# Down product of seven token pairs in a seven-product form with shared block sums, under a new instruction order

## The chip, the cores and the metric

The kernel runs on one core of one Trainium2 chip. The metric is the device time of one execution in microseconds, median of several runs; smaller is better. A core has a matrix engine (TensorE, PE in the profile, its weight loads PEld), three engines for elementwise work (VectorE or DVE, ScalarE or ACT, GpSimd or POOL) and SyncE (SP), which in this kernel only issues DMAs. Each engine runs its own list of instructions in order; they meet through semaphores.

## The reference, cut to what matters

One transformer block on 2048 tokens of width 640, in bfloat16: a layer norm, linear attention with 32 heads of 20 (a learned feature map `w_phi`, softmax of plus and minus the scores), an output product, a residual, a second layer norm, and a gated bilinear feed-forward of width 1536 with a second residual.

```python
qkv   = layernorm(x) @ wqkv                       # 640 -> 3*640
phi_q = [softmax(q w_phi), softmax(-q w_phi)]     # per head; phi_k alike
kv, z = phi_k^T v, sum(phi_k)                     # per head, over the tokens
h     = x + ((phi_q kv) / (phi_q z + 1e-6)) @ wo
y     = layernorm(h)
out   = h + ((y @ w_gate) * (y @ w_up)) @ w_down  # 640 -> 1536 -> 640
```

The change is in the last product, `(...) @ w_down`, and in the order in which all the work is issued.

## The kernel before, in words

Tokens are worked in 16 tiles of 128. Everything is emitted as small *units*, each with a name; a unit holds one or several operations on one or several engines. The names that matter here:

- Loads on SP: `in` (seven in SP's list, in this order of the program: two loads of the key weights into `phiqT`, the transposed token tiles 0 and 1 into `xT`, the value weights into `Wp`, the transposed token tiles 2 and 3), `lT4` to `lT15` (the other transposed token tiles), `lx0` to `lx3` (the tokens untransposed, four tiles each), `lwq` (the query weights into the buffer that held the key weights), `t0` to `t4` (transposed query weights), `lwo`, `lg`, `lu`, `ld` (output, gate, up and down weights). Two further `in` loads are on ACT's list: the last two fifths of the key weights, and `Wrows` (the feature map).
- Preparation of weights: `wk` (transposes of the key weights on PE, ten PE operations, with copies on DVE and ACT), `x0` to `x4` (key weights times feature map), `wv` and `c0` to `c4` (value weights centred), `wm`, `wq`, `y0` to `y4` (the same for the queries).
- Per token tile: `s` (statistics of the layer norm, in batches named by their first tile: `s0` is tiles 0 and 1, `s2` is tiles 2 and 3, `s4`, `s8`, `s12` four tiles each), `k`/`K` (key features), `v` (values), `A` (the sums over tokens), `q`/`Q` (query features, two DMA transposes each), `n` and `h` (attention output, output product and second layer norm), `f` (gate and up product of one of 12 feature blocks for four tiles).
- The down product: tiles 0 and 1 by the plain product (`d0`, `d1`), the other fourteen tiles in seven pairs `Db.i` (group of four tiles b, pair i). A pair is a 2-by-2 block product (two token tiles; features 0 to 767 and 768 to 1535; output columns 0 to 319 and 320 to 639), done with seven block products of six matmuls each instead of eight. Before it, `S` units form sums of blocks of the activations on DVE (`block_sums`, line 1101) and `T` units form sums of blocks of `w_down` on POOL, once for the whole kernel (`weight_sums`, line 1086).

In `down_pair` (line 1131) products accumulate in four PSUM banks; ACT copies a bank out (`snap`, line 1159), POOL adds copies to one another and to the residual `x_all` (`padd`, line 1165), DVE makes the last addition into the output tile (`fin`, line 1170), and SP stores it (`store`, line 1176).

The order on each engine is written out in `ORDER` as a list of unit names, one list per engine. `place` (line 213) takes the head of each list in turn, assigns buffers and fills DMA rings of eight slots; an engine's instructions are emitted in exactly the order of its list, SP's DMAs too. A load may be given a landing time with `at=`; `place` then takes that number for its landing, whatever its position in the list:

```python
land = o.at or max(s + 2.3, fabric) + o.bytes
...
load_wnat(1, (0, 1), at=2.9)
load_wnat(1, (1, 3), at=5.05)
load_xT(0, 5.35)
load_xT(1, 5.95)
load_wv(0, 5, 9.15)
for t, at in ((2, 9.1), (3, 9.8)):
    load_xT(t, at)
```

No wait in the emitted program depends on those numbers; each operation waits for the semaphores of what it reads (`finish`, line 302). `lwq` overwrites what `wk` reads, so its DMA is issued once the last `wk` transpose has been done. All matmuls are emitted from one helper (line 604), plain loads from line 497, transposing DMAs from line 501.

Of the kernel before, what the change touches and what calls it, by code (L numbers as in the profile page):

```python
# [472 lines left out]

# [845 lines left out]
```

## Time and profile before

| | |
|---|---|
| time, median of 3 runs | 276.26 us (276.13 to 276.52) |
| profiled execution: span from first to last instruction | 274.3 us |
| profiled execution: its own time | the page gives the span alone |
| PE busy | 266.2 us, 97% of the span |
| DVE, ACT, POOL busy | 202.0, 145.9, 147.9 us |
| granted TensorE clock | full in all 40 slices |
| DMA | 28.61 MB, busiest up to 60 us |

A span is shorter than the time by what lies around the first and last instruction. The profile page lists busy time by engine, 40 slices of the span, the DMA queues, the chain of work that ended last, groups of instructions and DMA issues by kind. A row of the timeline is: start in us, length in us, engine, source line, operation, what it writes and reads, shape, how many instructions are merged in it, and the idle time before it with what ended that. SPq and ACTq are the instruction streams that issue DMAs; their rows give the time that issuing takes, and "to landing" is from the issue to the semaphore. Matmuls are pipelined, so the length of a merged row is longer than the pitch of its matmuls by the drain of the last.

### The profile page before, as it was taken

To read this page: it belongs to the slowest core of one execution; us is meant where nothing else is said; L and a number is where in the kernel's file an instruction comes from. 1 tells how busy PE (TensorE), PEld (TensorE's weight loads), DVE (VectorE), ACT (ScalarE), POOL (GpSimd) and SP (SyncE) were. 2 spreads that over 40 slices of the span, in tenths; PEclk is the share of its full clock that TensorE was granted. 3 is DMA by queue.
4 is the path that set the end of the run, shared out by engine and by line. 5 is a ranking of instruction groups with operands and counts; after the bars stand their busy time and mean duration, and the time that the engine had idled before them with its cause. 6 is when DMAs were issued, how large, how long until landed. Compare 5 with 4: busy or idle time off the path is not lost.

```text
span 274.3 us, 5648 instructions
## 1 busy us (share of the span) xinstructions
PE 266.2 (97%) x2217; PEld 181.0 (66%) x2229; DVE 202.0 (74%) x388; ACT 145.9 (53%) x270; POOL 147.9 (54%) x187
## 2 busy tenths in 40 slices
PE   8999999999999999999999999999999999999992
PEld 8777776767868788788645557754554654456771
DVE  2899999999999989999855958555544565316772
ACT  3469999999676964776273422143342312332430
POOL 5437999999842365624899511621035330024895
PEclk9999999999999999999999999999999999999999
DMA  7988899803275897555564242620015101000112
GB/s 195 284 150 196 136 302 399 290 2 53 55 107 115 255 200 118 114 100 69 83 130 22 50 84 50 143 50 0 0 24 98 48 0 50 1 0 25 50 49 72
DMA packets 67099, 28.61 MB, mean 104 GB/s; under 512 B 57600, under 2 KB 65792, under 8 KB 67072
## 3 DMA queue, kind: packets, MB, share of 16 engines
q1 hardware_dynamic: 66144, 27.90, 44.9%
q10 hardware_dynamic: 928, 0.35, 0.5%
q8 instruction: 17, 0.28, 0.5%
q14 instruction: 10, 0.08, 0.1%
HBM read 11.82 MB, written 2.62 MB: 53 GB/s over the span
## 4 chain that ended last, share of the span: by engine, by line
PE 83%; POOL 6%; DVE 4%; DMA 2%; issue 2%; SPq 1%; ACT 1%; POOLq 0%; DVEq 0%
PE ps L604 83%; POOL eq L1167 4%; DMA Wp<-in_A_wqkv_dram 2%; POOL t L1167 2%; DVE ps L872 1%; DVE Sq L934 1%; SPq L501 1%; ACT phik L880 1%; DVE Ssum L894 0%; PE ps L512 0%; DVE Rk L896 0%; POOLq L371 0%; DVE x_all L1039 0%; DVE Phi L984 0%; SPq L497 0%
## 5 line engine op out<-in xcount | busy, mean ns | idle before, releaser
L604 PE MATMUL ps<-phik,Wgu 128*128 128x512 bf16 (+1 forms) x588 | 107.8, 335 | 0.6
L604 PEld LDWEIGHTS ps<-phik,Wgu 128*128 128x128 bf16 x600 | 58.1, 98 | 42.5 <-DVE phik L1079 1.2
L604 PE MATMUL ps<-Wp,xT 128*128 128x320 bf16 (+3 forms) x522 | 76.6, 299 | 0.2 <-ACT phik L880 0.2
L604 PEld LDWEIGHTS ps<-Wp,xT 128*128 128x128 bf16 x522 | 49.8, 98 | 19.5 <-ACT phik L880 0.7
L1079 DVE TENSOR_TENSOR phik<-ps,gate 128x512 bf16<-128x512 f32 (+1 forms) x60 | 34.0, 576 | 36.4 <-PE ps L604 29.9
L1077 ACT ACTIVATE gate<-ps 128x512 bf16<-128x512 f32 (+1 forms) x60 | 30.0, 511 | 53.8 <-PE ps L604 44.7
L897 POOL TENSOR_TENSOR phik<-phik,Rk 128x1280 bf16<-128x1280 bf16 x16 | 37.6, 2363 | 3.8 <-DVE Rk L896 3.0
L1167 POOL TENSOR_TENSOR eq<-eq 128x320 f32<-128x320 f32 x15 | 13.2, 881 | 33.1 <-ACT eq L1161 32.6
L872 DVE TENSOR_REDUCE ps<-ps 128x1 f32<-128x640 f32 (+1 forms) x32 | 26.1, 821 | 0.9 <-PE ps L604 0.3
L1161 ACT ACTIVATE eq<-ps 128x320 f32<-128x320 f32 x27 | 11.8, 438 | 27.0 <-PE ps L604 27.0
L1110 DVE TENSOR_TENSOR xT<-phik 128x768 bf16<-128x768 bf16 x35 | 23.7, 698 | 3.1 <-PE ps L604 3.1
L934 DVE TENSOR_REDUCE Sq<-eq 128x66 f32<-128x1320 bf16 x16 | 24.2, 1513 | 0.0
L894 DVE TENSOR_REDUCE Ssum<-phik 128x64 f32<-128x1280 bf16 x16 | 23.4, 1468 | 0.4 <-ACT phik L880 0.4
L1057 POOL TENSOR_SCALAR vpe<-shc 128x1 f32<-128x1 f32 x14 | 2.7, 192 | 36.4 <-ACT junk L597 36.1
L946 POOL TENSOR_TENSOR eq<-eq,rq 128x660 bf16<-128x660 bf16 x16 | 21.0, 1314 | 1.2
L597 ACT ACTIVATE junk<-x_all,nmh 128x640 bf16<-128x640 bf16 x14 | 11.6, 827 | 16.0 <-DVE x_all L1053 15.9
L880 ACT ACTIVATE eq<-ps,nb,rs 128x300 bf16<-128x300 f32 (+2 forms) x26 | 17.0, 687 | 5.4 <-DVE nb L875 4.6
L941 POOL TENSOR_TENSOR rq<-Sq,rq 128x33 f32<-128x33 f32 x16 | 4.5, 283 | 24.4 <-DVE rq L940 24.4
L604 PE MATMUL ps<-xT 128*128 128x320 bf16 (+1 forms) x144 | 17.4, 266 | 0.0
L880 ACT ACTIVATE eq<-ps,nb,nrs 128x300 bf16<-128x300 f32 (+2 forms) x26 | 17.2, 693 | 0.0
L880 ACT ACTIVATE phik<-ps,nb,rs 128x640 bf16<-128x640 f32 x16 | 14.2, 890 | 2.7 <-DVE nb L875 2.6
L604 PEld LDWEIGHTS ps<-xT 128*128 128x128 bf16 x144 | 11.8, 98 | 3.9 <-DVE xT L1110 0.2
(110 smaller groups left out, 374.9 us busy)
## 6 DMA issues: line engine op xcount, KB each, us to landing
x_all<-in_A_x_dram SPq DMA_DIRECT2D x4, 640.0 KB, 10.5
out_dram<-outb SPq DMA_DIRECT2D x16, 160.0 KB, 1.8
Wgu<-in_B_w_gate_dram SPq DMA_DIRECT2D x1, 1920.0 KB, 10.4
Wgu<-in_B_w_up_dram SPq DMA_DIRECT2D x1, 1920.0 KB, 15.8
vaug<-in_B_w_down_dram SPq DMA_DIRECT2D x1, 1920.0 KB, 9.0
Wp<-in_A_wqkv_dram SPq DMA_DIRECT2D x1, 800.0 KB, 4.9
phiqT<-in_A_wqkv_dram SPq DMA_DIRECT2D x1, 800.0 KB, 6.6
Wo<-in_A_wo_dram SPq DMA_DIRECT2D x1, 800.0 KB, 6.0
```

The lines of the kernel that those rows point to most:

```text
L604: ins = e.matmul(o_, lhsT=l_, rhs=r_, start=s_, stop=p_, skip_group_check=True)
L872: g.op("DVE", lambda e: e.tensor_reduce(out=mx(), in_=src(), axis=AX.XY if len(src().shape) == 3 else AX.X, op=ALU.max, apply_absolute_val ...
L880: g.op("ACT", lambda e, s=s, sc=sc, to=to, of=of: e.activation(out=to(s), in_=of(), func=ACT.Exp, bias=nb[:, i:i + 1], scale=sc[:, t:t + 1 ...
L894: g.op("DVE", lambda e: e.tensor_reduce(out=Ssum[:, vs.i, :], in_=x, axis=AX.X, op=ALU.add), rd=R_phik[t], wr=vs.R, use=[vs], t=1.39, lat=1.5)
L897: g.op("POOL", lambda e: e.tensor_tensor(out=x, in0=x, in1=Rk[:, vr.i, :].unsqueeze(2).to_broadcast([P, 2 * H, DH]), op=ALU.mult), rd=vr.R ...
L934: g.op("DVE", lambda e: e.tensor_reduce(out=Sq[:, vs.i, :].rearrange("p (w g) -> p w g", w=NQ), in_=feat(0, NQ).rearrange("p w (g f) -> p ...
L946: return e.tensor_tensor(out=x, in0=x, in1=rq[:, vr.i, :].rearrange("p (w h) -> p w h", h=HW).unsqueeze(3).to_broadcast([P, NQ, HW, DH]), ...
L1077: g.op("ACT", lambda e: e.activation(out=gate[:, vg.i, 0:P * n], in_=PS[v.i][:, 0, 0:P * n], func=ACT.Copy), rd=[v.R[0]], wr=vg.R, use=[v, ...
L1079: g.op("DVE", lambda e: e.tensor_tensor(out=hhT[:, hb, ft, sl], in0=PS[v.i][:, 1, 0:P * n], in1=gate[:, vg.i, 0:P * n], op=ALU.mult), rd=[ ...
L1110: g.op("DVE", lambda e, k=k, x=x, y=y, op=op: e.tensor_tensor(out=SH[k][i], in0=part(x), in1=part(y), op=op), rd=rd, wr=[R_S[k][i]], t=0.6 ...
L1161: o = g.op("ACT", lambda e: e.activation(out=slot(x), in_=PS[v.i][:, bk, 0:HALF], func=ACT.Copy), rd=[v.R[bk]], wr=x.R, use=[v, x], after= ...
L1167: g.op("POOL", lambda e: e.tensor_tensor(out=slot(o_), in0=slot(a), in1=in1(), op=op), rd=a.R + r_, wr=o_.R, use=[o_, a] + ([y] if x is No ...
```

## The change

The seven products of a pair are formed from other block sums. Each pair has four sums of activation blocks instead of five, two of them made from another sum, and there are four sums of weight blocks instead of five, two of them made from another sum. A pair's results are accumulated in three PSUM banks across products, with copies taken on the way: four copies by ACT instead of five, each followed by one POOL addition of `x_all` (four POOL additions instead of six), and four last additions by DVE, each of which reads a bank and one copy. The second tile of the pair is stored before the first. The number of products (seven) and of matmuls (42) per pair is the same. The `S` and `T` buffers move within `xT` and `Wp`. The dummy activation that loads ACT's table now uses the `junk` buffer's pool.

All five lists in `ORDER` are new. In SP's list the seven `in` loads stand at places 7, 8, 14, 23, 25, 27 and 29 of the list instead of 1 to 7. In ACT's list the `Wrows` load stands behind a first `wk` copy, and the table activation behind `x4`. `d0` and `d1` stand on PE ahead of the second half of the group `f0`; the last pair is D3.0 instead of D3.1.

```diff
     "PE":
-        "warm wk wk wk wk wk wk wk wk wk wk s0 s0 x1 x1 x3 wv wv x2 x0 x0 s2 s2 x4 k0 k0 k0 k0 k0 k3 k1 wm v2 k2 s4 v0 s4 s4 s4 "
+        "warm wk wk wk wk wk wk wk wk wk wk s0 s0 x1 x1 x3 wv wv x2 x0 x0 x4 s2 s2 k0 k0 k0 k0 k0 k1 k3 wm k2 s4 s4 s4 s4 k7 k4 "
...
-        "D3.0 D2.1 D3.0 D2.1 D2.1 D3.0 D3.0 D3.0 D3.1 D3.0 D3.1 D3.0 D3.1 D3.1 D3.1 D3.1 D3.1",
+        "f3.10.0 D2.0 D2.0 f3.6.0 f3.4.0 f3.4.0 D2.0 D2.0 D2.0 D2.0 f3.6.0 D2.1 D2.0 D2.1 D2.1 D3.1 D2.1 D2.1 D2.1 D3.1 D2.1 D3.1 "
+        "D3.0 D3.1 D3.1 D3.1 D3.1 D3.0 D3.0 D3.0 D3.0 D3.0 D3.0",
     "DVE":
...
+        "f3.10.0 S2.0.3 D2.0 S2.1.0 f3.4.0 D2.0 f3.6.0 D2.0 S2.1.2 S3.0.0 D2.0 S3.0.2 S2.1.3 S3.0.3 S3.1.0 D2.1 S3.0.1 S3.1.2 "
+        "D2.1 D2.1 D2.1 S3.1.1 S3.1.3 D3.1 D3.1 D3.1 D3.1 D3.0 D3.0 D3.0 D3.0",
     "ACT":
-        "in in in wk wk wk x2 x0 x4 k0 k0 wm k3 k3 v2 k1 k1 v0 k2 k2 wq3 wq1 v3 k7 k7 v7 y2 k4 k4 s12 v5 s12 v4 s12 y0 k6 k6 k5 "
+        "in wk in wk wk x2 x0 x4 in s12 k0 k0 k1 wm wo1 k1 k3 k3 k2 k2 wq1 s12 v2 wo1 v3 k7 v7 k7 k4 k4 k6 v5 k6 wq3 v0 s12 v1 y4 "
...
     "SP":
-        "in in in in in in in lwq t4 lT7 lT4 t2 lT5 lT6 t3 t1 t0 lx3 lT10 lT15 lT9 lT11 lT8 lT13 lT14 lT12 lx0 lwo lg lu lx2 "
-        "lx1 Q0 Q0 Q1 Q1 Q2 Q2 Q3 Q3 Q5 n2 Q5 n3 Q7 Q7 ld Q4 Q4 h2 h3 n5 Q6 Q6 n7 Q8 n4 Q8 n6 Q10 Q10 Q9 n8 Q9 h4 h5 h7 h6 Q12 "
...
+        "lx3 t2 t4 lT5 lT6 lwo in in lwq lT4 t0 lT7 lx1 in t1 lT9 lT8 lT11 lT10 lT15 lT13 t3 in lT12 in lT14 in lu in lg Q0 lx0 "
+        "Q0 lx2 Q1 Q1 Q2 Q2 Q3 Q3 Q5 Q5 n2 n3 Q7 Q7 ld Q4 Q4 n7 Q6 Q6 Q8 Q8 h2 n5 n6 n4 Q10 Q10 n8 h3 h7 Q9 Q9 h5 Q14 Q14 h6 h4 "
...
-    R_T, R_S = regs(5), [regs(2) for _ in range(5)]
+    R_T, R_S = regs(4), [regs(2) for _ in range(4)]
...
-    g.op("ACT", lambda e: e.activation(out=junk[:, 0, 0:1], in_=ones[:, 0:1], func=ACT.Exp), rd=[R_one], wr=[R_tab], t=1.4)
+    g.op("ACT", lambda e: e.activation(out=junk[:, 0, 0:1], in_=ones[:, 0:1], func=ACT.Exp), rd=[R_one], wr=[R_tab],
+         use=[Buf(p_junk)], t=1.4)
...
     def weight_sums():
...
-        for k, (a, b, op) in enumerate(((0, 3, ALU.add), (1, 3, ALU.subtract), (2, 0, ALU.subtract), (0, 1, ALU.add), (2, 3, ALU.add))):
+        for k, (a, b, op) in enumerate(((1, 0, ALU.subtract), (3, 1, ALU.subtract), (3, (0,), ALU.subtract), (2, (2,), ALU.subtract))):
...
     def block_sums(b, i):
...
-        for k, (x, y, op) in enumerate(((0, 3, ALU.add), (2, 3, ALU.add), (0, 1, ALU.add), (2, 0, ALU.subtract), (1, 3, ALU.subtract))):
+        for k, (x, y, op) in enumerate(((2, 3, ALU.add), (0, 2, ALU.subtract), ((0,), 0, ALU.subtract), (1, (2,), ALU.subtract))):
...
+        def snap(v, bk, t, half):
             x = Buf(p_slot)
...
+            x.read = g.op("ACT", lambda e: e.activation(out=slot(x), in_=PS[v.i][:, bk, 0:HALF], func=ACT.Copy), rd=[v.R[bk]],
+                          use=[v, x], t=0.42, lat=0.55, **rw)
+            g.op("POOL", lambda e: e.tensor_tensor(out=slot(x), in0=slot(x), in1=x_all[:, t, c], op=ALU.add), rd=x.R + [R_h[t]],
+                 wr=x.R, use=[x], t=0.87)
+            return x
...
-        padd(s4, s4, s5, ALU.subtract)
-        padd(s5, s4, None, x=(t1, 0))
-        padd(s1, s1, s4)
-        padd(s1, s1, None, x=(t2, 1))
-        padd(s1, s1, c12)
-        padd(s1, s1, c21, ALU.subtract)
-        fin(v1, 0, o1_, t1, s5)
+        mm(v1, 0, raw(0), wraw(0), True, [v2])
+        a_ = snap(v1, 0, t1, 0)
+        mm(v2, 0, summed(0), wsum_(0), True)
+        d_ = snap(v2, 0, t2, 1)
+        mm(v1, 0, summed(2), wsum_(2), False)
+        b_ = snap(v1, 0, t1, 1)
+        mm(v1, 1, raw(1), wraw(2), True)
+        fin(v1, 1, o1_, 0, a_)
+        mm(v1, 0, summed(1), wsum_(1), False)
+        c_ = snap(v1, 0, t2, 0)
+        fin(v1, 0, o2_, 1, d_, [c_])
+        mm(v2, 1, raw(3), wsum_(3), True)
+        fin(v2, 1, o2_, 0, c_)
+        store(o2_, t2)
+        mm(v2, 0, summed(3), wraw(3), False)
+        fin(v2, 0, o1_, 1, b_)
         store(o1_, t1)
-        fin(v2, 1, o2_, t2, s1)
-        store(o2_, t2)
...
-    g.alias(R_T, R_Wp[1] + R_Wp[2] + R_xT[0:6])
+    g.alias(R_T, R_Wp[1] + R_Wp[2] + R_xT[0:3])
...
-    g.alias([r for x in R_S for r in x], R_xT[5:])
+    g.alias([r for x in R_S for r in x], R_xT[2:12])
```

More of the change, by code (lines that the diff above doesn't have):

```diff
@@ L58 @@
 ST_ACT = (12,)
+SNAP = {}
 SPLIT = [[(0, 2), (2, 2)], [(0, 4)], [(0, 4)], [(0, 4)]]
@@ L143, in __init__ @@
         self.R = [Reg() for _ in range(nreg)]
+        self.read = None
 class Op:
@@ L465, in _build @@
     Wkv = Wp[:, :, D:3 * D]
-    TW = [Wkv[:, 0:3, 0:2 * HALF], Wkv[:, 0:3, 2 * HALF:4 * HALF], Wkv[:, 3:5, 0:3 * HALF],
-          xTf[:, 0:KH * HALF].rearrange("p (a n) -> p a n", a=3), xTf[:, KH * HALF:2 * KH * HALF].rearrange("p (a n) -> p a n", a=3)]
-    o1 = 2 * KH * HALF
+    TW = [Wkv[:, 0:3, 0:2 * HALF], Wkv[:, 3:5, 0:3 * HALF], Wkv[:, 0:3, 2 * HALF:4 * HALF],
+          xTf[:, 0:KH * HALF].rearrange("p (a n) -> p a n", a=3)]
+    o1 = KH * HALF
     SH = [[xTf[:, o1 + KH * P * (2 * k + i):o1 + KH * P * (2 * k + i + 1)].rearrange("p (f n) -> p f n", f=KH) for i in range(2)]
-          for k in range(5)]
+          for k in range(4)]
     PS = [ctx.enter_context(nc.psum_tensor("ps%d" % i, [P, 2, 512], FP32)) for i in range(4)]
@@ L1087, in weight_sums, with part @@
         lo, hi = (0, HALF), (HALF, D)
-        for k, (a, b, op) in enumerate(((0, 3, ALU.add), (1, 3, ALU.subtract), (2, 0, ALU.subtract), (0, 1, ALU.add), (2, 3, ALU.add))):
-            U("T%d" % k)
-            def part(q, n):
-                f0, (c0, c1) = KH * (q // 2), (lo, hi)[q % 2]
-                return Wd[:, f0:f0 + KH, c0:c1].rearrange("p (a w) n -> p a w n", w=n)
-            def out_(n, k=k):
-                return TW[k].rearrange("p a (w n) -> p a w n", w=n)
+        def part(q, n):
+            if isinstance(q, tuple):
+                return TW[q[0]].rearrange("p a (w n) -> p a w n", w=n)
+            f0, (c0, c1) = KH * (q // 2), (lo, hi)[q % 2]
+            return Wd[:, f0:f0 + KH, c0:c1].rearrange("p (a w) n -> p a w n", w=n)
+        for k, (a, b, op) in enumerate(((1, 0, ALU.subtract), (3, 1, ALU.subtract), (3, (0,), ALU.subtract), (2, (2,), ALU.subtract))):
+            U("T%d" % k)
             n = TW[k].shape[2] // HALF
-            pool_op(lambda e, a=a, b=b, op=op, n=n, part=part, out_=out_: e.tensor_tensor(out=out_(n), in0=part(a, n), in1=part(b, n), op=op),
-                    4.0, rd=[R_Wd], wr=[R_T[k]])
+            rd = [R_Wd] + ([R_T[b[0]]] if isinstance(b, tuple) else [])
+            pool_op(lambda e, k=k, a=a, b=b, op=op, n=n: e.tensor_tensor(out=part((k,), n), in0=part(a, n), in1=part(b, n), op=op),
+                    4.0, rd=rd, wr=[R_T[k]])
     def block_sums(b, i):
@@ L1104, in part @@
         def part(q):
+            if isinstance(q, tuple):
+                return SH[q[0]][i]
             f0, c = KH * (q % 2), c0 + P * (q // 2)
             return hhT[:, hb_, f0:f0 + KH, c:c + P]
-        for k, (x, y, op) in enumerate(((0, 3, ALU.add), (2, 3, ALU.add), (0, 1, ALU.add), (2, 0, ALU.subtract), (1, 3, ALU.subtract))):
+        for k, (x, y, op) in enumerate(((2, 3, ALU.add), (0, 2, ALU.subtract), ((0,), 0, ALU.subtract), (1, (2,), ALU.subtract))):
             U("S%d.%d.%d" % (b, i, k))
-            rd = [R_hhT[hb_][ft][2 * i + q // 2] for q in (x, y) for ft in range(KH * (q % 2), KH * (q % 2) + KH)]
+            rd = [R_hhT[hb_][ft][2 * i + q // 2] for q in (x, y) if not isinstance(q, tuple)
+                  for ft in range(KH * (q % 2), KH * (q % 2) + KH)] + [R_S[q[0]][i] for q in (x, y) if isinstance(q, tuple)]
             g.op("DVE", lambda e, k=k, x=x, y=y, op=op: e.tensor_tensor(out=SH[k][i], in0=part(x), in1=part(y), op=op),
@@ L1157, in slot @@
             return eqf[:, HALF * x.i:HALF * (x.i + 1)] if x.i < 6 else t32[:, x.i - 6, :]
-        def snap(v, bk):
+        how = iter(SNAP.get((b, i), "AAAA"))
+        def snap(v, bk, t, half):
             x = Buf(p_slot)
-            o = g.op("ACT", lambda e: e.activation(out=slot(x), in_=PS[v.i][:, bk, 0:HALF], func=ACT.Copy), rd=[v.R[bk]], wr=x.R,
-                     use=[v, x], after=SLOT_USERS, t=0.42, lat=0.55)
-            return x, o
-        def padd(o_, a, y, op=ALU.add, x=None):
-            r_, in1 = (y.R, lambda: slot(y)) if x is None else ([R_h[x[0]]], lambda: x_all[:, x[0], HALF * x[1]:HALF * (x[1] + 1)])
-            g.op("POOL", lambda e: e.tensor_tensor(out=slot(o_), in0=slot(a), in1=in1(), op=op), rd=a.R + r_, wr=o_.R,
-                 use=[o_, a] + ([y] if x is None else []), t=0.72)
@@ L1170, in fin @@
-        def fin(v, bk, o_, t, y=None, after=()):
-            in1 = (lambda: slot(y)) if y is not None else (lambda: x_all[:, t, HALF * bk:HALF * (bk + 1)])
-            g.op("DVE", lambda e: e.tensor_tensor(out=outb[:, o_.i, HALF * bk:HALF * (bk + 1)], in0=PS[v.i][:, bk, 0:HALF], in1=in1(),
-                                                  op=ALU.add), rd=[v.R[bk], R_h[t]] + (y.R if y is not None else []), wr=[o_.R[bk]],
-                 use=[v, o_] + ([y] if y is not None else []), after=after, t=0.45, lat=0.57)
+            c = slice(HALF * half, HALF * (half + 1))
@@ new lines, in snap @@
+            rw = dict(wr=x.R, after=SLOT_USERS)
+            if next(how) == "V":
+                g.op("DVE", lambda e: e.tensor_tensor(out=slot(x), in0=PS[v.i][:, bk, 0:HALF], in1=x_all[:, t, c], op=ALU.add),
+                     rd=[v.R[bk], R_h[t]], use=[v, x], t=0.45, lat=0.57, **rw)
+                return x
+            x.read = g.op("ACT", lambda e: e.activation(out=slot(x), in_=PS[v.i][:, bk, 0:HALF], func=ACT.Copy), rd=[v.R[bk]],
+                          use=[v, x], t=0.42, lat=0.55, **rw)
@@ new lines, in snap, with fin @@
+            g.op("POOL", lambda e: e.tensor_tensor(out=slot(x), in0=slot(x), in1=x_all[:, t, c], op=ALU.add), rd=x.R + [R_h[t]],
+                 wr=x.R, use=[x], t=0.87)
+            return x
+        def fin(v, bk, o_, half, y, after=None):
+            g.op("DVE", lambda e: e.tensor_tensor(out=outb[:, o_.i, HALF * half:HALF * (half + 1)], in0=PS[v.i][:, bk, 0:HALF], in1=slot(y),
+                                                  op=ALU.add), rd=[v.R[bk]] + y.R, wr=[o_.R[half]], use=[v, o_, y],
+                 after=[x.read for x in after or () if x.read], t=0.45, lat=0.57)
@@ L1178, in store @@
                  t=0.6, lat=0.3, size=0.4)
-        mm(v1, 1, summed(2), wraw(3), True, [v2])
-        s5, _ = snap(v1, 1)
-        mm(v2, 0, raw(3), wsum_(2), True)
-        s4, _ = snap(v2, 0)
-        mm(v1, 0, summed(0), wsum_(0), True)
-        s1, _ = snap(v1, 0)
-        mm(v1, 1, raw(0), wsum_(1), False)
-        c12, a12 = snap(v1, 1)
-        fin(v1, 1, o1_, t1, after=[a12])
-        mm(v2, 0, summed(1), wraw(0), False)
-        c21, a21 = snap(v2, 0)
-        fin(v2, 0, o2_, t2, after=[a21])
-        mm(v1, 0, summed(4), wsum_(4), False)
-        mm(v2, 1, summed(3), wsum_(3), True)
-        padd(s4, s4, s5, ALU.subtract)
-        padd(s5, s4, None, x=(t1, 0))
-        padd(s1, s1, s4)
-        padd(s1, s1, None, x=(t2, 1))
-        padd(s1, s1, c12)
-        padd(s1, s1, c21, ALU.subtract)
-        fin(v1, 0, o1_, t1, s5)
+        mm(v1, 0, raw(0), wraw(0), True, [v2])
[14 more added lines that the diff above has]
+        fin(v2, 0, o1_, 1, b_)
         store(o1_, t1)
-        fin(v2, 1, o2_, t2, s1)
-        store(o2_, t2)
     def wqT(a):
```

83 rows, old and new, of the table ORDER are left out of this document.

## The prediction, made before the changed kernel was run

> **What bounds the kernel now.** I read the page first, then who waited on PE, then the stretches at the end, then SP's own rows at the start.
>
> ```profile
> span 274.3 us, 5648 instructions
> PE 266.2 (97%) x2217; PEld 181.0 (66%) x2229; DVE 202.0 (74%) x388; ACT 145.9 (53%) x270; POOL 147.9 (54%) x187
> ```
>
> PE is busy for 97% of the span. A busy PE can hide waits, so the second look is PE's waits between the first key product (12.6) and the last matmul (269):
>
> ```profile
> PE ps L512 <- DVE x_all L1039: 0.4, 1, 0.4
> PE ps L604 <- DVE Phi L987: 0.2, 1, 0.2
> PE ps L604 <- ACT phik L880: 0.2, 1, 0.2
> ```
>
> That is 0.8 us in 256. From 12.6 on the kernel is a solid block of matmuls; whatever is taken off DVE, ACT or POOL inside it is worth nothing, and whatever delays its beginning moves its end by the same amount. Time can change only ahead of the block and behind it. Behind it lie 5.2 us without a matmul:
>
> ```profile
> 269.10:274.30 5.20, 0.00 (x0) 0.00 (x0) 0.82 (x2) 0.00 (x0) 2.13 (x3) 1.00 0.18 63
> ```
>
> Ahead of it PE needs, in its list's order, the key weights, token tiles 0 and 1, the value weights, and tiles 2 and 3:
>
> ```profile
> 0.82 4.07 PE L604 MATMUL ps<-const-bfloat16-1.0 128*128 128x128 bf16 x38 [0.82 <-PEq L1304]
> 5.51 0.28 PE L604 MATMUL ps<-ones,phiqT 128*128 128x1 bf16 x5 [0.21 <-DMA phiqT<-in_A_wqkv_dram]
> 9.33 1.53 PE L604 MATMUL ps<-Wp,ones 128*128 128x320 bf16 x10 [0.31 <-DMA Wp<-in_A_wqkv_dram]
> 11.64 0.73 PE L604 MATMUL ps<-xT 128*128 128x129 bf16 x10
> 12.60 1.12 PE L604 MATMUL ps<-Wp,xT 128*128 128x320 bf16 x7
> ```
>
> The row at 11.64 is `s2`, which reads tiles 2 and 3; 12.60 is `k0`. All five loads come in time because they head SP's list:
>
> ```profile
> 0.79 0.88 SPq L497 DMA_DIRECT2D phiqT<-in_A_wqkv_dram  x2
> 1.72 2.61 SPq L501 DMA_TRANSPOSE xT<-in_A_x_dram  x2
> 4.37 0.59 SPq L497 DMA_DIRECT2D Wp<-in_A_wqkv_dram  x1
> 5.00 2.55 SPq L501 DMA_TRANSPOSE xT<-in_A_x_dram  x2
> 7.59 0.58 SPq L497 DMA_DIRECT2D phiqT<-in_A_wqkv_dram  x1
> 17.19 4.71 SPq L501 DMA_TRANSPOSE phiqT<-in_A_wqkv_dram  x3
> 21.95 0.58 SPq L497 DMA_DIRECT2D x_all<-in_A_x_dram  x1
> 22.58 10.70 SPq L501 DMA_TRANSPOSE xT<-in_A_x_dram  x8
> ```
>
> The reader is to see that issuing alone costs SP time: 10.70 / 8 = 1.34 us for each transposed tile, 4.76 / 3 = 1.59 for a transposed weight (17.19 to 21.95), 0.63 for a plain load (21.95 to 22.58). Landing takes longer still:
>
> ```profile
> vaug<-in_B_w_down_dram SPq DMA_DIRECT2D x1, 1920.0 KB, 9.0
> Wp<-in_A_wqkv_dram SPq DMA_DIRECT2D x1, 800.0 KB, 4.9
> phiqT<-in_A_wqkv_dram SPq DMA_DIRECT2D x1, 320.0 KB, 4.2
> xT<-in_A_x_dram SPq DMA_TRANSPOSE x16, 4.2
> ```
>
> **The head, step by step.** The new SP list starts lx3, t2, t4, lT5, lT6, lwo and only then the two key-weight loads. From 0.79: 0.63 + 2 x 1.59 + 2 x 1.34 + 0.63 puts the first at 7.9 and the second at about 8.5. Landing 4.2 later, and a little more behind the 800 KB of lwo, gives 13.0 (5.5 before). Next in the list is lwq, which overwrites what `wk` reads, so all of SP stands until PE is done with `wk`: before, 2.1 us from the landing (5.5 to 7.59). After eight idle us I let PE run as at the program's start, where 38 matmuls of 128 columns took 4.07, or 107 ns each. The same width took 56 ns later:
>
> ```profile
> 76.52 0.28 PE ps L512 x5
> ```
>
> Four rounds of five transposes then cost 20 x 0.051 = 1.0 more, so lwq issues at 16.1 (bounds 15.1, with no such slowing, to 16.5). Behind it, up to the last `in`, stand 13 token transposes (4, 7, tile 0, 9, 8, 11, 10, 15, 13, tile 1, 12, 14, tile 2), three weight transposes (t0, t1, t3) and four plain loads (lwq, lx1, the value weights, lu): 13 x 1.34 + 3 x 1.59 + 4 x 0.63 = 24.7. Tile 1 issues at 34.2 and lands near 38.4 (`s0` waits for it), the value weights issue at 36.9 and land at 41.8, lu issues at 40.2, and tile 3 at 40.8, straight behind the 1920 KB of lu. What that does is seen at the one other place where transposes follow a load of this size:
>
> ```profile
> 90.03 0.59 SPq L497 DMA_DIRECT2D vaug<-in_B_w_down_dram  x1
> L501 SPq DMA_TRANSPOSE phiqT<-eq x1: 2292/2292/2292, 92.1 to 92.1; - x1
> DMA to landing us min/median/max: 7.6/7.6/7.6
> ```
>
> The transpose issued at 92.1 took 7.6 us, landing at 99.7, 9.6 after the issue of the big load and 0.6 behind its landing (90.03 + 9.0). So tile 3 lands at 40.2 + 9.6 = 49.8. The other end is its own 4.2 us, 45.0; I take 49.8, the row of the same case. Then 0.05 to wake and half of `s2`, 0.28, and `k0` starts at 50.1 against 12.60: **+37.5 us**.
>
> The Trainium skill, "DMA: Bandwidth & Descriptors", section on queues, rings and completion order, says that completion is not FIFO per issuing engine: a later DMA may finish ahead of an earlier one. By that the landing of tile 3 could be the 45.0 end, the first rival below. The rows just shown speak against it here, as they show a transpose held until the big load was in.
>
> Does the clock cost again at 49.8? Ends: 0 (PE held full rate across its 0.31 wait at 9.33) and 2.0 (38 x 51 ns, the restart as at the program's start). Before `s2` PE has the value sums and four `x` groups to do from 41.8; at the slow rate they end near 47 (twice 1.53 less drain for the ten sums, twice about 0.3 for each group, which is what `x4` took between the end of `s2` and 12.60), so the wait is under 3 us behind 5 us of work. That is nearer to the 0.31 than to a cold start: 0. The Trainium skill, "TensorE: Matmul & The Clock Gate", Part 1, has the clock halved after an idle window of about 3.4 us; by that this wait might just keep the clock, and the sum would be the same or 2.0 more. No row here shows a long wait in mid-kernel.
>
> Other moves at the head cost nothing, as long as tile 3 is that late. The `Wrows` load on ACT now waits for a `wk` copy (about 15, +4.4 to land, so 20; its reader `x1` stands behind `s0` at 38). The table load and a first `s12` square on ACT end before the first exponentials, two us behind `k0`. lx0 and lx2 go behind `Q0`'s transposes, first at 61.30 before, so about 99 after; the add that first reads lx0 ran at 81.45, so about 119:
>
> ```profile
> 61.30 22.05 SPq L501 DMA_TRANSPOSE phiqT<-eq  x9
> 81.45 0.86 DVE x_all L1039
> ```
>
> **The block.** 42 matmuls a pair stay, and `d0` and `d1` move as they are: 0. Removed: 7 block sums on DVE (7 x 0.70 = 4.9), 14 of 42 POOL additions (14 x 0.88 = 12.3), 7 ACT copies (7 x 0.44 = 3.1), one weight sum (3.8):
>
> ```profile
> L1167 POOL TENSOR_TENSOR eq<-eq 128x320 f32<-128x320 f32 x15 | 13.2, 881 | 33.1 <-ACT eq L1161 32.6
> L1161 ACT ACTIVATE eq<-ps 128x320 f32<-128x320 f32 x27 | 11.8, 438 | 27.0 <-PE ps L604 27.0
> L1110 DVE TENSOR_TENSOR xT<-phik 128x768 bf16<-128x768 bf16 x35 | 23.7, 698 | 3.1 <-PE ps L604 3.1
> L1098 POOL TENSOR_TENSOR xT<-vaug x2: 3815/3818/3822, 102.6 to 147.2; 128x1920 bf16<-128x1920 bf16 x2
> ```
>
> All of it lies beside PE, whose waits there sum to 0.8 us, so the gain is 0 (at most 0.8). New waits: a third product into a bank must wait for ACT's copy of the second, some 0.7 behind its end, with one product (0.82) between them in the tightest place. I take 0, and 0 to 3 for the range (14 such places at 0.2). The new order's own stalls are unknown: -0.8 to +3, taken as 0.
>
> **The end.** Two terms. First, eight of the last block sums stand ahead of the one (S3.1.2) that PE wants some 8 us after the last `f`. Sums took 0.51 while POOL was still and 0.97 while it added:
>
> ```profile
> 253.16 1.02 DVE L1110 TENSOR_TENSOR xT<-phik 128x768 bf16<-128x768 bf16 x2
> 260.48 2.92 DVE L1110 TENSOR_TENSOR xT<-phik 128x768 bf16<-128x768 bf16 x3
> 262.00:269.10 7.10, 7.03 (x52) 4.74 (x50) 4.70 (x10) 2.35 (x6) 6.71 (x8) 1.00 0.14 47
> ```
>
> POOL was busy 6.71 of 7.1 there; with four additions for six I take two thirds of the slowing, 0.82 a sum, by which S3.1.2 is late by **+0.5** (0 to 1.7). Second, the tail:
>
> ```profile
> 267.23 1.80 PE L604 MATMUL ps<-xT 128*128 128x320 bf16 x12
> 269.59 1.80 POOL L1167 TENSOR_TENSOR eq<-eq 128x320 f32<-128x320 f32 x2
> 271.49 0.49 DVE L1172 TENSOR_TENSOR outb<-ps,eq 128x320 bf16<-128x320 f32 x1 [2.06 <-POOL eq L1167]
> ```
>
> Now PE ends at 269.03 and a string of POOL additions runs to 271.4 before the last DVE addition; the end is 5.2 behind PE. After, the fifth product's copy (0.44), one POOL addition (0.90) and two DVE additions (2 x 0.49), with 0.05 at each of three hand-overs, end 2.5 after that product; PE ends two products after it (1.6, the 1.80 row without its drain). The 0.9 between, and store and end as now (2.3, from 271.98), make 3.2. **-2.1** (-2.4 with that POOL addition hidden, -1.1 with another queued ahead of it).
>
> **Sum** against the profiled execution: 274.3 + 37.5 + 0.5 - 2.1 = 310.2 of span. Only the span is given for it; the median of the runs lies 2.0 above, so 312.2: **312 us**.
>
> **Rivals.** *Tile 3 overtakes lu.* It lands at 45.0. Then the value weights decide: landed at 41.8, sums and `x` groups until about 47, `s2`, `k0` at 47.4, which is +34.8, so 309.5; with PE at full rate `k0` comes at 45.3, 307.4. I say 308. For it: it is a small DMA. Against: the 92.1 row. *The block doesn't stay solid.* Restart at half rate (+2.0), the bank waits (+3.0) and late sums (+1.2): 318.4. For it: sums of 0.97. Against: the bank waits have a product between them. *The loads' order is free, not slower.* SP's 1.34 us would be back-pressure of transfers ahead rather than a price of issuing, so the list runs through at once and PE waits for nothing: 276.3 + 0.5 - 2.1 = 274.7. It decides where `k0` starts by 14.2, so tile 3 lands by 13.8, which needs the 28 entries ahead of it issued in 9 us, 0.32 each. Against it also stands the volume ahead of tile 3, 9.5 MB by the shapes, which at the 257 GB/s of the first 12 us is 37 us:
>
> ```profile
> 0.00:12.00 12.00, 10.65 (x151) 9.73 (x152) 5.91 (x17) 4.03 (x7) 6.91 (x27) 1.00 0.93 257
> ```
>
> **Chances.** Forecast 0.72, tile 3 overtaking 0.12, the loose block 0.13, a free order 0.02, anything that ends level 0.01. Runs agree within 0.2%, so I count a change beyond that. The range goes from the lower rival with an earlier lwq and a short tail (308 - 3.5) to the upper one: 304.5 to 318.5, since each term of the head is a sum of some twenty pitches and may be off by 3.
>
> **What would show it.** SP: lwq at about 16, tile 1 at 34, tile 3 at 41 landing near 50. PE: waits of some 8 us before `wk`, of 9 and 12 before the two halves of `s0`, of a few before `s2`, all put down to DMAs into `phiqT`, `xT` and `Wp`; `k0` near 50; from there waits of under 3 us in all; 3.2 us from the last matmul to the end. DVE 28 block sums, POOL 28 additions. Wrong would be: `k0` before 45, an lwq that doesn't wait for `wk`, or a mid-kernel wait above 3 us.

## The result and the profile after

The changed kernel takes 313.27 us (median of five runs, 312.49 to 313.87) against 276.24 (276.06 to 276.52): a ratio of 1.134, with a 95% interval of 1.1325 to 1.1358. The profiled execution took 312.76 us, of which 310.9 are its span.

The page of the changed kernel: span, busy time by engine, and the slices of PE and of the clock that it was granted.

```profile
span 310.9 us, 5582 instructions
PE 272.3 (88%) x2216; PEld 183.4 (59%) x2229; DVE 201.2 (65%) x381; ACT 141.9 (46%) x263; POOL 132.3 (43%) x172
PE   5310267999999999999998999999999999999996
PEclk9555559999999999999999999999999999999999
```

PE is idle through most of the first six slices (47 us) and solid from there on. The clock slices show 5 while it is idle. Who PE waited for, all waits of the changed kernel (total, times, longest):

```profile
PE ps L606 <- DMA xT<-in_A_x_dram: 20.9, 3, 10.0
PE ps L606 <- DMA phiqT<-in_A_wqkv_dram: 8.2, 1, 8.2
PE ps L606 <- DMA Wp<-in_A_wqkv_dram: 2.4, 1, 2.4
...
PE ps L606 <- DVE phik L1081: 0.5, 1, 0.5
PE ps L606 <- DVE Phi L989: 0.5, 1, 0.5
PE ps L606 <- DVE xT L1116: 0.4, 1, 0.4
PE ps L606 <- DVE ob L1023: 0.4, 1, 0.4
PE ps L606 <- DVE outb L1131: 0.3, 1, 0.3
PE ps L606 <- DVE outb L1182: 0.2, 1, 0.2
```

31.5 us are waits for three kinds of loads, all at the head; the six waits for DVE, 2.3 us, lie in the block. PE's timeline at the head, where each wait stands in its row's bracket:

```profile
13.19 0.29 PE L606 MATMUL ps<-ones,phiqT 128*128 128x1 bf16 x5 [8.16 <-DMA phiqT<-in_A_wqkv_dram]
13.35 0.69 PE L695 MATMUL ps<-ident,phiqT 128*128 128x128 bf16 x5
26.91 0.72 PE L606 MATMUL ps<-xT 128*128 128x129 bf16 x5 [10.03 <-DMA xT<-in_A_x_dram]
36.86 0.72 PE L606 MATMUL ps<-xT 128*128 128x129 bf16 x5 [9.23 <-DMA xT<-in_A_x_dram]
41.83 2.85 PE L606 MATMUL ps<-Wp,ones 128*128 128x320 bf16 x10 [2.44 <-DMA Wp<-in_A_wqkv_dram]
48.49 0.46 PE L606 MATMUL ps<-xT 128*128 128x129 bf16 x5 [1.64 <-DMA xT<-in_A_x_dram]
48.78 4.24 PE L606 MATMUL ps<-Wp,xT 128*128 128x320 bf16 x30
```

`k0` starts at 48.78 instead of 12.60. SP's rows of the same stretch, the times of issuing:

```profile
0.79 0.46 SPq L498 DMA_DIRECT2D x_all<-in_A_x_dram  x1
...
7.69 9.60 SPq L498 DMA_DIRECT2D phiqT<-in_A_wqkv_dram  x3
...
18.66 1.27 SPq L502 DMA_TRANSPOSE phiqT<-in_A_wqkv_dram  x1
...
24.60 7.89 SPq L502 DMA_TRANSPOSE xT<-in_A_x_dram  x6
...
39.69 0.58 SPq L498 DMA_DIRECT2D Wgu<-in_B_w_up_dram  x1
40.31 1.71 SPq L502 DMA_TRANSPOSE xT<-in_A_x_dram  x1
```

The row at 7.69 holds the two key-weight loads and `lwq`, with SP's standstill in it: 9.60 us for three issues of about half a us. The last row is tile 3. Its landing, from the view of its line in that moment, and then the last product in PE's timeline (start, duration; the span ends at 310.9):

```profile
DMA to landing us min/median/max: 8.1/8.1/8.1
```

```profile
306.86 0.98 PE L606 MATMUL ps<-vaug,xT 128*128 128x320 bf16 x6
```

Three numbers describe a run from here on. The *head* is the start of `k0`, the *block* runs from there to the end of the last matmul, the *tail* from there to the end of the span:

| | head | block | tail | span |
|---|---|---|---|---|
| before | 12.6 | 256.4 | 5.2 | 274.3 |
| after | 48.8 | 259.1 | 3.1 | 310.9 |
| difference | +36.2 | +2.6 | -2.1 | +36.7 |

### The profile page after: what moved, and what is told of

Read it like the earlier page. It is cut to its first block, busy times and chain, and to the rows that moved or that the text cites. A ratio compares the mean times of both kernels' runs of the same rounds, so it can differ in the third digit from the quotient of the medians.

```text
span 310.9 us, 5582 instructions
## 1 busy us (share of the span) xinstructions
PE 272.3 (88%) x2216; PEld 183.4 (59%) x2229; DVE 201.2 (65%) x381; ACT 141.9 (46%) x263; POOL 132.3 (43%) x172
## 4 chain that ended last, share of the span: by engine, by line
PE 76%; SPq 9%; DVE 6%; DMA 4%; issue 2%; POOL 1%; POOLq 0%; ACT 0%; DVEq 0%
PE ps L606 75%; SPq L502 8%; DMA xT<-in_A_x_dram 3%; DVE xT L1116 2%; DMA phiqT<-in_A_wqkv_dram 2%; SPq L498 1%; PE ps L695 1%; DVE outb L1182 1%; DVE phik L1081 1%; DVE ps L874 1%; POOL eq L1177 1%; DVE hb L1064 0%; DVE Sq L936 0%; PE ps L513 0%; POOLq L372 0%
## 5 line engine op out<-in xcount | busy, mean ns | idle before, releaser
L606 PE MATMUL ps<-Wp,xT 128*128 128x320 bf16 (+1 forms) x606 | 89.5, 299 | 0.8 <-DVE xT L1116 0.4
L606 PEld LDWEIGHTS ps<-Wp,xT 128*128 128x128 bf16 x606 | 57.4, 98 | 25.1 <-ACT vaug L905 0.8
L1177 POOL TENSOR_TENSOR eq<-eq,x_all 128x320 f32<-128x320 f32 x22 | 18.9, 867 | 65.1 <-ACT eq L1175 64.9
L606 PE MATMUL ps<-vaug,phik 128*128 128x63 bf16 (+1 forms) x308 | 26.1, 238 | 0.2 <-DVE outb L1182 0.2
L896 DVE TENSOR_REDUCE Ssum<-phik 128x64 f32<-128x1280 bf16 x16 | 23.4, 1472 | 0.0
L606 PE MATMUL ps<-xT 128*128 128x129 bf16 x60 | 4.9, 235 | 20.9 <-DMA xT<-in_A_x_dram 20.9
L606 PEld LDWEIGHTS ps<-vaug,phik 128*128 128x128 bf16 x308 | 18.4, 97 | 7.0 <-DVE outb L1182 0.7
L943 POOL TENSOR_TENSOR rq<-Sq,rq 128x33 f32<-128x33 f32 x16 | 4.2, 264 | 36.2 <-DVE rq L942 36.2
L1182 DVE TENSOR_TENSOR outb<-ps,eq 128x320 bf16<-128x320 f32 x22 | 10.3, 485 | 12.6 <-PE ps L606 8.1
L882 ACT ACTIVATE eq<-ps,nb,nrs 128x300 bf16<-128x300 f32 (+2 forms) x26 | 17.3, 696 | 0.0
L1175 ACT ACTIVATE eq<-ps 128x320 f32<-128x320 f32 x22 | 9.5, 435 | 17.0 <-PE ps L606 17.0
L606 PEld LDWEIGHTS ps<-xT 128*128 128x128 bf16 x60 | 4.0, 104 | 21.7 <-DMA xT<-in_A_x_dram 21.6
```

What stands on the lines that cost most here:

```text
L606: ins = e.matmul(o_, lhsT=l_, rhs=r_, start=s_, stop=p_, skip_group_check=True)
L882: g.op("ACT", lambda e, s=s, sc=sc, to=to, of=of: e.activation(out=to(s), in_=of(), func=ACT.Exp, bias=nb[:, i:i + 1], scale=sc[:, t:t + 1 ...
L896: g.op("DVE", lambda e: e.tensor_reduce(out=Ssum[:, vs.i, :], in_=x, axis=AX.X, op=ALU.add), rd=R_phik[t], wr=vs.R, use=[vs], t=1.39, lat=1.5)
L1177: g.op("POOL", lambda e: e.tensor_tensor(out=slot(x), in0=slot(x), in1=x_all[:, t, c], op=ALU.add), rd=x.R + [R_h[t]], wr=x.R, use=[x], t= ...
L1182: g.op("DVE", lambda e: e.tensor_tensor(out=outb[:, o_.i, HALF * half:HALF * (half + 1)], in0=PS[v.i][:, bk, 0:HALF], in1=slot(y), op=ALU. ...
```

## The experiments

The theory: SP issues in the order of its list, at about 1.3 us a transpose, stands still for `wk`, and so brings tile 3 in 38 us late; the rest of the change moves the time by little. Rivals were that other parts of the change hold some of the head, that transfers and not issuing bound it, and, for the 2.6 us in the block, that the new form or the late head makes them.

**e1. The old kernel with the new load order.**

```diff
     "SP":  (kernel before)
-  in in in in in in in lwq t4 lT7 lT4 t2 ... lx0 lwo lg lu lx2 lx1 Q0 Q0 Q1
+  lx3 t2 t4 lT5 lT6 lwo in in lwq lT4 t0 lT7 lx1 in t1 ... lT14 in lu in lg Q0 lx0 Q0 lx2 Q1
```

> The kernel before, with nothing changed but SP's list: its loads are put in the order of the changed kernel (lx3, t2, t4, ... lu, in, lg, then lx0 and lx2 between the transposes of Q0 and Q1). Theory A (the order of the loads on SP alone makes the time): the first key product starts at 48 to 50 us instead of 12.60, everything behind it keeps its pace, so 276.2 + 36 = 312, between 310 and 315. Rival B (a good part comes from ACT's list, where the feature-map load stands behind a copy, or from the new form of the down product): under 300, because ACT's list and the form are those of before here.

Measured: 314.48 us, ratio 1.139 (1.1355 to 1.1424). The old form of the down product, with its own four other lists, is as late as the changed kernel. So SP's list alone is enough for the whole loss. The rows of PE, and the stretch behind them (PE, PEld, DVE, ACT, POOL, then the granted clock):

```profile
49.05 0.46 PE L604 MATMUL ps<-xT 128*128 128x129 bf16 x5 [2.10 <-DMA xT<-in_A_x_dram]
...
49.73 5.85 PE L604 MATMUL ps<-Wp,xT 128*128 128x320 bf16 x30
```

```profile
48.00:60.00 12.00, 10.95 (x99) 7.85 (x100) 8.03 (x17) 6.00 (x9) 3.48 (x8) 0.86 0.48 175
```

30 matmuls took 5.85 here and 4.24 in the changed kernel: here the clock fell behind the 2.10 us wait, and 14% of 12 us, 1.7, is about what the block grew by (258.0 against 256.4). The tail is the old one, 5.2.

**e2. Key weights first.**

```diff
     "SP":  (changed kernel)
-  lx3 t2 t4 lT5 lT6 lwo in in lwq lT4 ...
+  in in lx3 t2 t4 lT5 lT6 lwo lwq lT4 ...
```

> The changed kernel with the two key-weight loads at places 1 and 2 of SP's list, the other 27 entries of the head in their new order. Theory A (SP's issuing is the bound of the head and stands still while it waits for wk): lwq, issued at 16.92 in the changed kernel, has no wait left and issues when its turn comes, at 0.8 + 3 x 0.5 + 2 x 1.3 + 1.8 + 1.3 + 0.6 = 8.6 or so; all behind it comes 8.3 earlier, k0 at 40.5, time 313.3 - 8.3 = 305. Rival C (the head is bound by the transfers and not by issuing, so time saved in issuing is lost in landing): a gain of under 4, so above 309.

Measured: 307.53 us, ratio 1.1155 (1.1113 to 1.1197), between the two. The profiled execution is the slowest of its four (309.84; the others 307.1 to 307.57), so its rows explain a gain of 2.9 us and not the median's 5.7; where the other runs gained more isn't shown. In it `lwq` came 6.9 earlier but `k0` only 4.4 (44.36), and about 1.5 of that went into a longer block (260.5), where 30 matmuls took 5.71 us instead of 4.24. SP's rows show where the other 2.5 stayed:

```profile
5.04 4.33 SPq L503 DMA_TRANSPOSE xT<-in_A_x_dram  x2
...
10.04 1.35 SPq L499 DMA_DIRECT2D phiqT<-in_A_wqkv_dram  x1
...
12.72 1.71 SPq L503 DMA_TRANSPOSE phiqT<-in_A_wqkv_dram  x1
14.47 2.35 SPq L503 DMA_TRANSPOSE xT<-in_A_x_dram  x1
```

Issuing isn't a fixed price. With several loads in flight a transpose took up to 3.0 us (one of the two in the first row) instead of 1.3, and the plain load `lwq` 1.35 instead of 0.37, so both theories hold a part: SP's list is the bound, and the transfers stretch it.

**e10. As e2, with lwo out of the clump.**

```diff
-  in in lx3 t2 t4 lT5 lT6 lwo lwq lT4 ... lT11 lT10 lT15 ...
+  in in lx3 t2 t4 lT5 lT6 lwq lT4 ... lT11 lT10 lwo lT15 ...
```

> As e2 (key weights first), with the load of the output weights (lwo) moved from place 8 to behind lT10. In e2 SP's rows between 5.0 and 16.8 were stretched (3.0, 1.35, 1.7 and 2.35 us in place of 1.3, 0.4, 1.3 and 1.3), with lx3, lwo and lwq in flight. Theory E (a clump of large loads in flight holds up issuing): with lwo out of the clump the three stretches behind it, 2.4 us together, go, and k0 comes near 42 instead of 44.4. Rival (the stretch belongs to the first 17 us whatever is in flight): k0 at 44.

`k0` came at 43.18, half way between the two numbers (a single run, 309.43 us). Its block is 261.3, 2.3 longer than in the changed kernel, and not by the clock: the 30 matmuls behind `k0` took 4.24, and the granted clock is full from there on. In it PE waited three times for DVE (1.39, 0.28 and 0.20 us) where the changed kernel has no wait. A part of the stretch went with the load: the rows of `t0` and `lT7` are back at 1.27 and 1.28, and new long ones stand behind `lwo` at its new place. Others stayed: `lT5` and `lT6` still took 3.65 together, and `lT4` behind `lwq` took 2.01.

```profile
12.55 1.28 SPq L503 DMA_TRANSPOSE xT<-in_A_x_dram  x1
...
22.34 0.58 SPq L499 DMA_DIRECT2D Wo<-in_A_wo_dram  x1
22.97 3.09 SPq L503 DMA_TRANSPOSE xT<-in_A_x_dram  x2
26.10 1.91 SPq L503 DMA_TRANSPOSE phiqT<-in_A_wqkv_dram  x1
```

So the stretch comes with loads in flight and not with the first 17 us alone, and moving the load moved a part of it: `k0` gained 1.2 us on e2. How many bytes in flight it takes isn't settled.

**e3. The up weights behind tile 3.**

```diff
-  ... lT14 in lu in lg
+  ... lT14 in in lu lg
```

> The changed kernel with the load of the up weights (lu) put behind token tile 3 in SP's list, all else the same. Theory A (a transpose behind a 1920 KB load lands when that load is in): tile 3 issues at 39.7 and lands at 43 to 44 instead of 48.4; then PE's value sums, which run at half rate until about 46.4, decide, k0 at 47.0 instead of 48.78: 313.3 - 1.7 = 311.6. Rival (tile 3 was late by its place alone): no change, 313.3 within 0.5.

Tile 3 issued at 39.7 again and landed 3.9 us later instead of 8.1:

```profile
L503 SPq DMA_TRANSPOSE xT<-in_A_x_dram x1: 1784/1784/1784, 39.7 to 39.7; - x1
...
DMA to landing us min/median/max: 3.9/3.9/3.9
```

`k0` started at 47.30 (expected 47.0). Here a transpose behind a 1920 KB load does wait for it. In the median only 0.6 us came of it (312.63, ratio 1.1306 to 1.139, overlapping the changed kernel's interval), because the block grew by 1.1 in the profiled execution, which has two waits of PE for DVE's gate products (1.3 us together) where the changed kernel has one of 0.5.

**e4. PE kept at work until the key weights come.**

```diff
-    warm(38)
+    warm(200)
```

> The changed kernel with 200 instead of 38 idle matmuls at the start, so that PE is at work until the key weights land near 13.2 to 14.0. Theory A (PE falls back to half rate while it waits, and that makes wk 1.0 longer, for which SP stands): the five-transpose rounds of wk take 0.4 instead of 0.67, lwq issues about 0.9 earlier than 16.92, and k0 and the end with it: 312.4. Rival (the half rate has no part in it): 313.3 within 0.3.

Inconclusive in time: 314.02 us, spread over 313.1 to 316.6. The rounds of `wk` did take 0.40 (15.82 to 16.22) instead of 0.67:

```profile
15.82 0.27 PE L606 MATMUL ps<-ones,phiqT 128*128 128x1 bf16 x5
...
16.22 0.27 PE L606 MATMUL ps<-ones,phiqT 128*128 128x1 bf16 x5
```

But the first round began at 14.55 instead of 13.19, on a load that landed that much later in this run, so `lwq` issued no earlier (17.2). Why the load was later isn't known. The 200 matmuls themselves ended only at 14.33, so with the load on time the round would have been 1.1 us late all the same: this run can't price the half rate.

**e5. All seven loads first on SP, ACT's list as changed.**

```diff
-  lx3 t2 t4 lT5 lT6 lwo in in lwq lT4 t0 lT7 lx1 in ...
+  in in in in in in in lx3 t2 t4 lT5 lT6 lwo lwq lT4 t0 lT7 lx1 ...
```

> The changed kernel with the seven in loads at places 1 to 7 of SP's list, all else as changed (ACT's list too, where the feature-map load stands behind a wk copy). Theory A: tile 3 is in at 10.5 as in the kernel before; what is left of the late head is the feature map, issued near 6.9 and in near 10, by which the x groups come some 4 us later than before: k0 at 16 to 17 instead of 48.78, time 313.3 - 32.3 = 281, between 279 and 283. Rival B (something other than SP's order holds a good part of the head): above 290.

Measured: 284.34 us, ratio 1.0291 (1.027 to 1.0313). Of the 37 us 29 are back; the time is 1.3 above the range. The head is 19.5 rather than 16 to 17: the feature map, moved on ACT, now shows, as the prediction had it hidden only behind the late tile 3.

```profile
12.99 0.76 PE L607 MATMUL ps<-Phi,phiqT 128*128 128x140 bf16 x6 [5.14 <-DVE Phi L586]
...
14.74 2.87 PE L607 MATMUL ps<-Wp,ones 128*128 128x320 bf16 x10
```

After 5.14 us without work PE came back at half rate: 2.87 us for the value sums that took 1.53 before, and the `x` groups around them likewise, some 2 us in all. The block is 260.2, 1.1 longer than in the changed kernel, with a new wait of 0.95 for the query weights.

**e6. The whole head of loads as before.** SP's list up to `Q0` and the first three entries of ACT's are those of the kernel before; two `s12` and two `wo1` on ACT stand later, behind their loads.

> The changed kernel with the whole head of loads as in the kernel before: SP's list up to Q0 from there, the three in entries first on ACT, and on ACT two s12 squares and two wo1 sums moved back to behind their loads. Theory A: k0 at 12.6 as before, so 313.3 - 36.2 = 277.1, up to 279 where token tiles come later than the new PE order wants them. The block of matmuls from k0 to the last one was 259.1 long in the changed kernel and 256.4 in the one before. If that excess belongs to the new order or the new form it stays, and the time is at or above 277. Rival (the excess came from the late head): the block shrinks to 256.4, and with a tail of 3.1 the time is 274.3.

Measured: 281.80 us, ratio 1.0229 (1.019 to 1.0268). `k0` is at 12.67, as said; the time is above the range. The block is 263.4, 4.3 more than in the changed kernel. The new PE order counts on loads that all came in during the long head; with `k0` at 12.7 it runs into them and into ACT, with waits of 2.9 us in all that the changed kernel's block doesn't have; the rest of the 4.3 isn't traced. Two of these waits:

```profile
20.53 0.74 PE L607 MATMUL ps<-xT 128*128 128x129 bf16 x10 [0.84 <-DMA xT<-in_A_x_dram]
...
39.18 0.49 PE L607 MATMUL ps<-Phi,phiqT 128*128 128x140 bf16 x6 [0.62 <-ACT vaug L906]
```

The rival (a block of 256.4 once the head is early) falls.

**e7. The new form in the old order.**

The edit: all five lists of the kernel before, without S*.4 and T4, and without one ACT copy and two POOL additions per pair; the weight sums in the sequence T0 T2 T3 T1, the sums of a pair in the sequence 0 2 1 3.

> The new form of the down product in the order of the kernel before: all five lists from there, with the surplus entries taken out (one block sum, one ACT copy and two POOL additions per pair, one weight sum) and the remaining sums put in the sequence in which the new products need them. Theory A (the form alone gives the tail, 5.2 to 3.2 us behind the last matmul, and nothing else): block 256.4, time 276.1 - 2.1 = 274.0. Rival (the 2.7 us by which the block grew belong to the form, through its waits between products and copies): 276.7.

Measured: 275.21 us, ratio 0.9965 (0.9953 to 0.9977): faster than before, by a third of a percent. Head 12.7, tail 3.1, block 257.2. The 0.8 too much is one wait, made by where the sums were put: S2.1.3 overwrites what the last product of D1.1 reads, waited for it, and held DVE's next gate product.

```profile
229.71 1.47 PE L607 MATMUL ps<-phik,Wgu 128*128 128x512 bf16 x6 [0.64 <-DVE phik L1082]
```

**e9. e7 with that sum moved.**

```diff
     "DVE":
-  ... S2.1.1 D1.1 S2.1.3 S2.0.3 f3.4.0 D1.1 f3.11.0
+  ... S2.1.1 D1.1 f3.4.0 D1.1 S2.1.3 S2.0.3 f3.11.0
```

> The new form in the order of the kernel before, with one mend: the last block sums of pairs 2.1 and 2.0 (S2.1.3, S2.0.3) stand behind f3.4.0 and the last addition of D1.1 on DVE. In e7 S2.1.3 stood ahead and waited 2.5 us for the last product of D1.1, which still reads its buffer, and PE lost 0.8 at 229.7 to the f3.4.0 held behind it. Theory: that wait goes, block 256.4 + 0.1, tail 3.1, time 275.2 - 0.8 = 274.4, a ratio to the kernel before near 0.994. Rival (the wait moves on to the next sum): 275.2.

Measured: **274.21 us**, ratio 0.9927 (0.9914 to 0.9939). The block is 256.4, the tail 3.1. This version beats both kernels, the one before by 0.7%. PE's block is as long as in the kernel before, and the rows of POOL, PE and DVE at the end show why the tail is short: one addition, under the last product, where there was a string of them.

```profile
268.11 0.79 POOL L1178 TENSOR_TENSOR eq<-eq,x_all 128x320 f32<-128x320 f32 x1 [0.84 <-ACT eq L1176]
...
268.21 0.98 PE L607 MATMUL ps<-vaug,xT 128*128 128x320 bf16 x6
269.01 0.89 DVE L1183 TENSOR_TENSOR outb<-ps,eq 128x320 bf16<-128x320 f32 x2 [0.39 <-POOL eq L1178]
```

**e8. d0 and d1 late again.**

```diff
     "PE":  (changed kernel; DVE and SP alike)
-  ... q14 n4 n6 d0 h5 n8 q11 q12 h6 d1 h4 f0.5.2 ... h15 f2.4.0 f1.5.0 D0.1
+  ... q14 n4 n6 h5 n8 q11 q12 h6 h4 f0.5.2 ... h15 d0 d1 f2.4.0 f1.5.0 D0.1
```

> The changed kernel with d0 and d1 moved back to behind the group f1 on PE, DVE and SP, all else the same. The block from k0 to the last matmul was 259.1 there against 256.4 before, and four of its waits lie in the 12 us behind d1 (on DVE's outb, phik and ob; 1.9 us of lost PE time together). Theory D (the two early plain products load DVE where it is fullest and hold PSUM banks): these four waits go, the block is 257.2 or so. Rival (the order of q, h, n and f there makes them, d1 or not): only the wait on outb goes, block 258.6. The two waits of 0.97 together near the end stay in both. The time of single runs spreads by over 1 us here, so the block is read from the trace.

Both were wrong: 325.11 us, ratio 1.1758 (1.174 to 1.1776). The block is 271.7 in the profiled execution (326.72), 12.6 more than with the early `d0` and `d1`. Two of the four waits (on `outb`, 0.31, and on `ob`, 0.40) did go with them, but larger ones came, which they had filled:

```profile
158.92 4.18 PE L607 MATMUL ps<-phik,Wgu 128*128 128x256 bf16 x20 [2.44 <-DMA phik<-hb]
...
165.68 2.35 PE L607 MATMUL ps<-phik,Wgu 128*128 128x256 bf16 x20
...
172.44 1.11 PE L607 MATMUL ps<-phik,Wgu 128*128 128x256 bf16 x5 [2.25 <-DVE phik L1082]
```

Without those 6.5 us of work PE waits 2.44 for the transposed `hb`, and loses its clock by it: the twenty matmuls behind take 4.18, against 2.35 for the next twenty of that kind. Waits in the block are 9.6 us instead of 2.3, and nearly all the rest of the 12.6 is half rate. About 1.5 of that has nothing to do with `d0` and `d1`: it follows a wait of 1.93 us just ahead of `k0`.

## Why the prediction was right

The time came out at 313.3 for 312, by the mechanism that was forecast and through its terms. Two of them, head and block, missed in opposite directions (-1.3 and +2.1), so that the sum came closer than its parts was luck.

- **The head, +37.5 forecast, +36.2 measured.** The key weights landed at 13.2 and near 14.0 (13.0 forecast); `wk` ran at half rate, as assumed, its five transposes in 0.69; `lwq` ended its issue at 17.3, so it issued at 16.9 (16.1). From there to tile 3 it took 23.4 (24.7): a weight transpose takes 1.3 and not 1.59, which I had from a row of three with a stretched one in it. lu and tile 3 behind it landed 8.3 and 8.1 after their issues, 0.7 to 0.9 us sooner than by the row of the down weights. e1 shows that the list of SP is enough for all of it, e3 that the place behind lu was worth 4.2 us of landing.
- **The clock behind the last wait, 0.** In the profiled execution it held (30 matmuls in 4.24). It was the weakest step: my reason, a wait under 3 us behind 5 us of work, doesn't carry. In e1 a wait of 2.10 lost it, for 1.7 us. The 0 was right for a wait of 1.64, and it was luck: in e2 and e4 waits of 1.90 and 1.94 at the same place cost the clock.
- **The block, +0.5 forecast, +2.6 measured.** This is the term that was mis-sized. The late sums near the end cost 1.0 rather than 0.5, by the starts of the products that wait there (296.08, 297.50 and 298.70, where six matmuls have a pitch of 0.81). The 1.6 beyond that belong to the new order, which I had put at 0 with bounds of -0.8 to +3: most of it is in four waits of 0.3 to 0.5 us, three of them between 158 and 169, where the block before has three in all, of 0.2 to 0.4. e7 and e9 show that the new form has no part in it (block 256.4 in the old order) and e1 that the late head has none beside the clock. What in the new order makes the waits between 158 and 169 isn't settled; e8 shows only that without the early `d0` and `d1` there are longer ones.
- **The tail, -2.1 forecast, -2.1 measured**, and again in e7 and e9.
- **Nothing for the removed work.** 7 block sums, 14 POOL additions, 7 copies and a weight sum left the block as long as it was: e9 is faster than before by the tail alone.

Of the rivals, the free order fell with e1 and e5. Tile 3 overtaking lu fell with the row of 8.1 and with e3. The section on completion order in "DMA: Bandwidth & Descriptors" of the Trainium skill allows it; no run here shows it. Of the loose block the late sums came true in part (1.0 of 1.7); the restart at half rate did not happen in the changed kernel's profiled execution, but in those of e1, e2, e4 and e8.

## What to carry to other kernels

A queue's order counts to its last needed entry: look for the first wait that the compute engine cannot pass, count what stands ahead of it in the issuing engine's list (issue pitch, standstills, large transfers just ahead), and ignore what a planner's own landing times say about it (9.8 us for tile 3 here, which landed at 48.4). Price a form and an order apart: here the new form in the old order was worth -0.7% (e9), and the order that came with it cost 14% on top of that. A piece of work that looks badly placed may be filling a hole, so move it before judging it.

## What the runs showed of the hardware that was not expected

The clock fell after waits well under 3 us. It held across 1.64 (changed kernel) and was lost with 1.90 (e2), 1.94 (e4), 2.10 (e1), and 1.93, 2.25 and 2.44 (e8), after which matmuls ran at half rate for 3.41 us. The Trainium skill, "TensorE: Matmul & The Clock Gate", Part 1, gives an idle window of about 3.4 us for it; here shorter waits did it.

The traces show more than the length of the wait. In all of them the time between two changes of the granted clock is a whole number of steps of 3.41 us (eleven at half rate in the changed kernel's head, 8.31 to 45.86). First the step of e1 in which PE waited 2.10 us and the next one, then the step of the changed kernel with the 1.64 us (PE, PEld, DVE, ACT, POOL, then the granted clock):

```profile
46.16:49.58 3.42, 1.32 (x24) 1.15 (x22) 1.41 (x3) 1.10 (x2) 0.00 (x0) 1.00 1.07 379
49.58:52.99 3.41, 3.41 (x18) 2.02 (x16) 1.42 (x5) 0.70 (x1) 0.43 (x2) 0.50 1.02 398
```

```profile
45.86:49.27 3.41, 1.77 (x27) 1.48 (x25) 2.60 (x4) 2.38 (x6) 0.00 (x0) 1.00 1.08 380
```

PE was busy for 39% of the step ahead of e1's fall and for 28 to 45% ahead of those of e2, e4 and e8; in the changed kernel it was 52%, and the clock held. These figures suggest that the cost of a wait hangs on how much work shares its step, and so on where the step begins, which differs from run to run. Where the limit lies isn't settled: at the very end of e3, a step with 44% of work kept the clock. The mean granted clock of a run says little of these losses: the changed kernel's run at 1.0 took 313.87 us, the one at 0.94 that was profiled 312.76.

Issue time on SP is not constant: 1.3 us for a transpose in a quiet queue, 1.7 to 3.0 with loads of 640 to 800 KB in flight (e2, e10).

A block sum of 768 columns on DVE took 0.55 us alone and 1.04 to 1.14 beside POOL's additions in the changed kernel, and two of those additions took 2.17 there (0.79 for one alone). The Trainium skill, "GPSIMD Engine Reference", Specifications, has the two engines share their SBUF interface, with contention when a DVE instruction has two inputs there; these rows agree:

```profile
294.46 0.55 DVE L1116 TENSOR_TENSOR xT<-phik 128x768 bf16<-128x768 bf16 x1
...
296.30 1.14 DVE L1116 TENSOR_TENSOR xT<-xT,phik 128x768 bf16<-128x768 bf16 x1
```

```profile
295.92 2.17 POOL L1177 TENSOR_TENSOR eq<-eq,x_all 128x320 f32<-128x320 f32 x2
```
